# Value products as two 64-column halves and output transposes as four 64x64 tiles, in a delta-rule plus mixture-attention kernel

## Chip, core and metric

The kernel runs on one core of one Trainium2 chip, as one launch. Times are device microseconds. The time before is the median of three runs.

## What is computed

Inputs q, k, v have shape (4 batches, 8 heads, 768 positions, 48), beta (4, 8, 768). The first stage is a recurrence per batch and head (k normalized, state 48x48), the second a mixture of four causal attentions whose weights come from a top-2 gate:

```python
for t in range(S):                       # delta rule, per batch and head
    y[t] = q[t] @ state
    state = state + beta[t] * outer(k_n[t], v[t] - k_n[t] @ state)
x = y with the heads side by side        # (4, 768, 384)
logits = x @ w_gate                      # (384, 4), the two largest chosen
for e in range(4):
    q, k, v = x @ wq[e], x @ wk[e], x @ wv[e]      # 64 wide
    a = exp(causal(q @ k.T / 8) - rowmax); a /= a.sum() + 1e-9
    out += gate[e] * (a @ v @ wo[e])     # gate 0 where e was not chosen
```

## The kernel before

The work is cut into six units (n = 0 to 5): two batches at a time, three stretches of 256 positions each. s = n % 3 is the place of the stretch in the sequence, so attention in a unit covers s + 1 stretches of keys and the units grow: 0, 1, 2, then again 3, 4, 5 for the other two batches.

A unit goes through these stages. The recurrence is done in chunks of 64 positions: Gram products of keys (`gk`, `gq`), a triangular solve done step by step on VectorE and GpSimd (`pre`, `sv`, lines 420 and 422), then per chunk `ks`, `ex`, `uu`, `eu`, `yu`, `yq`, `st`, `es`. Those small products use the TensorE array as four 64x64 tiles in turn, in the order of rows and columns (0,0), (1,1), (0,1), (1,0). The outcome x is kept transposed in `xh`. The projections `pj` and `pv` are 128x128 products. The attention of a unit is, per batch b, pair of experts y and key stretch kp:

- `mx`, `em`: scores with queries as rows, for the row maxima; `mp`, `mr`, `er` turn the maxima over.
- `sc`: scores with keys as rows and queries as columns, in PSUM; the two experts of a pair are the two row halves of the array (64x128 tiles).
- `xp`: the exponential on ScalarE (line 743) into one of three tiles `at` (128 keys x 2 experts x up to 512 columns of queries).
- `av`: the product by values. The stationary operand is a 128x128 block of `at` (keys x queries), the moving one the 128x65 block of values `vs` (64 columns and a column of ones, which gives the row sum). The result, 128 queries x 65, is accumulated over key blocks in one PSUM bank, for two experts x and two query halves i side by side.
- `oa` copies the sums out to `os`, `nm` (line 760 on) turns row sums and gates into factors, `on` (line 765) multiplies.
- `ft`: transposes of `on` by a product with an identity, so that queries lie in columns; row half r of the queries goes to PSUM bank r. `fh`, `fl` split the result into a rounded part and a rest, `fo` applies wo in three 128x128 products, `eo` and `do` send it out.

Both `at`, `vs` and `on` are plain float32 tiles. A float32 product shows in the profile as two matmuls and two weight loads, so the 336 products of `av` are 672 and the 96 of `ft` are 192. The products that read float32r tiles (`pj`, `pv`, `sc`, `mx`, `fo`) show once.

The order of all steps on every engine is written out by hand in one long list of words, `ORDER`; each word calls one function with its arguments, the last digit after the colon being the PSUM buffer (four buffers of two banks). TensorE, VectorE, ScalarE and GpSimd each take their instructions in that order. All products go through one helper, `mm` (line 182), so that in the profile they are told apart by their tiles: `ps<-vs,at` is `av`, `ps<-cst,on` is `ft`, `ps<-kq` is `gk` and `gq`, `ps<-on,os` is a step of the first unit's solve that uses two 64x64 tiles in turn, rows 0-63 with columns 0-63 and rows 64-127 with columns 64-127.

In the order, the steps `av` form 27 groups on TensorE. Six of them follow, and seven precede, a step of full 128x128 products (`pj`, `pv`, `fo`, `fill`); the other neighbours use half tiles.

Of the kernel before, what the change touches and what calls it, by code (L numbers as in the profile page):

```python
# [23 lines left out]
SIDES = (slice(0, 64), slice(64, 128))  # L24
# [148 lines left out]
def tile_kernel(ctx, tc, kq, kv, beta, wqk, wvg, wo, consts, out):  # L173
# [7 lines left out]
    def mm(o, a, b, start, stop=True):  # L181
        T.matmul(o, lhsT=a, rhs=b, start=start, stop=stop, skip_group_check=True)  # L182
# [14 lines left out]
    def two(k):  # L197
        return PP[int(k)]
# [15 lines left out]
    id64 = cst[:, 0:64]  # L214
# [19 lines left out]
    VS = cp.tile([128, 2, 6, NE, EH + 1], F32, name="vs")  # L234
# [12 lines left out]
    ON = cp.tile([128, 2, NE, EH], F32, name="on")  # L247
# [415 lines left out]
    FOUR = ((0, 0), (1, 1), (0, 1), (1, 0))  # L663
# [81 lines left out]
    def av(n, b, y, kp, k):  # L745
        s = n % 3
        A = at_of(n, b, y, kp)
        O = two(k)[:, 0, 0:260].rearrange("p (x i d) -> p x i d", x=2, i=2)
        for j in range(2):
            for x in range(2):  # L750
                for i in range(j if kp == s else 0, 2):
                    o = 256 * j + 128 * i - (128 if kp == s and j else 0)
                    mm(O[:, x, i], A[:, x, o:o + 128], VS[:, b, 2 * kp + j, 2 * y + x], kp == j == x == i == 0)

    def oa(n, b, y, e, k):
        cpy(e, OS[b][:, 2 * y:2 * y + 2].rearrange("p x i d -> p (x i d)"), two(k)[:, 0, 0:260])
# [11 lines left out]
    def ft(n, b, k):  # L768
        for i in range(2):
            for x in range(2):  # L770
                for r in range(2):
                    w = 128 * i + 64 * x
                    mm(two(k)[:, r, w:w + 64], ON[SIDES[r], i, 2 * x:2 * x + 2].rearrange("p e d -> p (e d)"), id64[SIDES[r]], True)

    fv = lambda k: two(k)[:, :, 0:256].rearrange("p r (q t) -> p q r t", q=4)
    ov = lambda x: x.rearrange("p i x (r t) -> p (i x) r t", r=2)
# [103 lines left out]
```

## Time and profile before

| | |
|---|---|
| median of 3 runs | 488.77 us (484.72 to 489.02) |
| the profiled execution's own time | 488.29 us |
| its span, first to last instruction | 486.4 us |
| TensorE matmuls, busy | 433.9 us, 9543 instructions |
| VectorE, ScalarE, GpSimd busy | 313.6, 182.3, 170.8 us |
| mean granted TensorE clock | 0.959 |

"PE" is TensorE's matmul stream and "PEld" its weight loads; the two overlap. A group's busy time is the union of its instructions, while the length of one matmul is mostly latency, since matmuls are pipelined: the pace of a stream is read from the starts. The timeline view merges neighbouring instructions of one kind: "start, length, engine, line, operation, tiles, shape, count", and "128*128" ahead of a shape is the part of the array in rows * columns.

### The profile page before, as it was taken

Reading aid. Unit: us, or ns where it says so; the run is one execution under the profiler, and the core shown is the slowest. Engines: PE = TensorE matmul, PEld = TensorE weight load, DVE = VectorE, ACT = ScalarE, POOL = GpSimd, SP = SyncE. Lnnn points to the kernel's source line nnn. Section 1 sums busy time; section 2 is a strip of 40 time slices with the busy share of each in tenths; the row PEclk is TensorE's granted clock in tenths of the full one; section 3 lists DMA queues with packets and bytes.
Section 4 is the critical chain, followed back from the end, with each engine's and each line's share of the span. In section 5 each row is a group of like instructions: output and inputs, shape, how many; then the busy total and the mean of one; then the engine's idle time right before and its main releaser. Section 6 shows DMA issues by size and latency. Waiting matters only on the chain.

```text
span 486.4 us, 21099 instructions
## 1 busy us (share of the span) xinstructions
PE 433.9 (89%) x9543; PEld 396.1 (81%) x9543; DVE 313.6 (64%) x655; ACT 182.3 (37%) x349; POOL 170.8 (35%) x314
## 2 busy tenths in 40 slices
PE   5529888878999889998999999999999989999995
PEld 4529777867888769897888989999887879999994
DVE  3996769766679894776667485775677764642011
ACT  2516233532325542364352354173531122323331
POOL 1505744544474462404146342744601000011000
PEclk9999999868999996998699999999999989999999
DMA  8920343211303151120035120011403000000001
GB/s 187 236 71 13 91 119 102 49 36 47 105 11 107 34 167 52 52 67 1 3 100 150 35 53 1 1 36 37 144 16 110 19 3 18 2 34 15 20 1 66
DMA packets 15435, 29.33 MB, mean 60 GB/s; under 512 B 2801, under 2 KB 8945, under 8 KB 15345
## 3 DMA queue, kind: packets, MB, share of 16 engines
q1 hardware_dynamic: 15088, 27.59, 20.7%
q8 instruction: 75, 1.23, 1.1%
q10 hardware_dynamic: 256, 0.39, 0.3%
q14 instruction: 16, 0.12, 0.1%
HBM read 20.89 MB, written 4.72 MB: 53 GB/s over the span
## 4 chain that ended last, share of the span: by engine, by line
PE 71%; DVE 15%; DMA 4%; ACT 4%; issue 3%; SPq 1%; POOL 1%; DVEq 0%; ACTq 0%; POOLq 0%
PE ps L182 71%; DMA at<-in_wvg_dram 2%; ACT tt L186 1%; DVE bl L420 1%; DVE mx L684 1%; DVE tp L422 1%; DMA kq<-in_kq_dram 1%; DMA kv<-in_kv_dram 1%; DVE tn L452 1%; DVE ql L619 1%; SPq L596 1%; DMA xh<-xh 1%; DVE tt L190 1%; DVE xb L538 1%; DVE xh L590 1%
## 5 line engine op out<-in xcount | busy, mean ns | idle before, releaser
L182 PE MATMUL ps<-vs,at 128*128 128x65 f32 x672 | 80.1, 276 | 0.1
L182 PEld LDWEIGHTS ps<-vs,at 128*128 128x128 f32 x672 | 77.3, 192 | 1.8 <-ACT at L743 0.4
L422 POOL TENSOR_TENSOR tp<-bl 128x238 f32<-128x238 f32 (+13 forms) x90 | 44.0, 489 | 89.3 <-DVE bl L420 80.6
L743 ACT ACTIVATE at<-ps 128x768 f32<-128x768 f32 (+1 forms) x48 | 43.8, 919 | 50.0 <-PE ps L182 49.8
L684 DVE TENSOR_REDUCE mx<-ps 128x2 f32<-128x1024 f32 (+3 forms) x48 | 44.8, 952 | 13.9 <-PE ps L182 13.6
L420 POOL TENSOR_TENSOR bl<-bl,tp 128x238 f32<-128x238 f32 (+13 forms) x90 | 47.1, 523 | 7.1
L182 PE MATMUL ps<-kq 48*64 48x64 f32 x1536 | 38.2, 243 | 12.0 <-DVE tt L348 4.8
L182 PE MATMUL ps<-xh,wqkh 128*128 128x256 f32 x288 | 45.5, 294 | 2.9 <-DMA xh<-xh 1.8
L182 PEld LDWEIGHTS ps<-kq 48*64 48x64 f32 x1536 | 32.4, 154 | 16.0 <-issue 6.6
L182 PEld LDWEIGHTS ps<-xh,wqkh 128*128 128x128 f32 x288 | 38.6, 194 | 4.9 <-issue 2.0
L186 ACT ACTIVATE tt<-ps 32x256 f32<-32x256 f32 (+2 forms) x87 | 33.4, 384 | 17.1 <-PE ps L182 10.7
L182 PE MATMUL ps<-qh,kh 64*128 64x256 f32 x192 | 35.1, 357 | 1.1 <-DVE sb L562 1.1
L182 PE MATMUL ps<-kh,qh 64*128 64x512 f32 (+3 forms) x128 | 26.8, 439 | 3.5 <-DVE kl L619 2.1
L182 PE MATMUL ps<-ql,kh 64*128 64x256 f32 x192 | 28.2, 285 | 0.0
L182 PEld LDWEIGHTS <-ide 64*128 64x128 bf16 (+1 forms) x479 | 23.3, 103 | 5.9 <-issue 1.2
L182 PE MATMUL ps<-qh,kl 64*128 64x256 f32 x192 | 28.0, 283 | 0.0
L182 PE MATMUL ps<-mr,sel 64*128 64x256 bf16 x192 | 27.3, 276 | 0.0
L182 PE MATMUL ps<-wvgh,xh 128*128 128x260 f32 x144 | 25.4, 303 | 1.4 <-DVE pm L356 1.4
L182 PE MATMUL ps<-mask,ide 64*128 64x128 bf16 (+1 forms) x384 | 26.4, 217 | 0.0
L765 POOL TENSOR_TENSOR on<-os,rsm 128x512 f32<-128x512 f32 x9 | 9.4, 1048 | 46.1 <-DVE rsm L762 46.1
L182 PE MATMUL ps<-xh,wqkl 128*128 128x256 f32 x144 | 25.4, 286 | 0.0
L182 PEld LDWEIGHTS ps<-wvgh,xh 128*128 128x128 f32 x144 | 21.2, 204 | 2.0 <-DVE pm L356 1.6
(197 smaller groups left out, 915.9 us busy)
## 6 DMA issues: line engine op xcount, KB each, us to landing
kv<-in_kv_dram SPq DMA_DIRECT2D x24, 384.0 KB, 3.7
kq<-in_kq_dram SPq DMA_DIRECT2D x40, 192.0 KB, 3.6
out_dram<-ot SPq DMA_DIRECT2D x12, 384.0 KB, 2.9
xh<-xh SPq DMA_DIRECT2D x72, 32.0 KB, 2.5
kq<-in_kq_dram SPq DMA_DIRECT2D x12, 96.0 KB, 3.9
at<-in_wqk_dram SPq DMA_DIRECT2D x3, 256.0 KB, 3.8
kq<-in_kq_dram ACTq DMA_DIRECT2D x4, 96.0 KB, 4.0
at<-in_wvg_dram SPq DMA_DIRECT2D x1, 256.0 KB, 7.6
```

Of the source, the lines that this page charges most:

```text
L182: T.matmul(o, lhsT=a, rhs=b, start=start, stop=stop, skip_group_check=True)
L186: S.activation(o, x, AF.Copy, **({} if scale is None else {"scale": scale}))
L190: V.tensor_scalar(o, x, scale, None, op0=OP.mult)
L420: e.tensor_tensor(X[:, a:b, i + 1:], X[:, a:b, i + 1:], tv, op=OP.subtract)
L422: e.tensor_tensor(tv, R[:, :, i + 1:].to_broadcast([128, w, m]), X[:, a:b, i:i + 1].to_broadcast([128, w, m]), op=OP.mult)
L452: V.transpose(TN[n % 2].rearrange("p t l -> p l t"), BB[n % 2])
L538: V.tensor_tensor(XB.rearrange("p (a b) d -> p a (b d)", a=2), kv_of(n, c)[:, 1].rearrange("p (a b) d -> p a (b d)", a=2), ax(k), op=OP.su ...
L590: V.tensor_tensor(x, y, yv(n, c, k, 0)[0], op=OP.subtract)
L596: nc.sync.dma_start(x[r + HD:r + 64, :, i].bitcast(F32), x[r + 16 * i:r + 16 * i + 16, :, 3].bitcast(F32))
L684: V.tensor_reduce(d, two(k)[:, :, a:a + 128 * (k1 - k0)], axis=AX.X, op=OP.max)
L743: S.activation(at_of(n, b, y, kp)[:, :, 0:w], two(k)[:, :, 0:w], AF.Exp, scale=0.125)
L765: (V, G)[e - 1].tensor_tensor(ON, OS[b][:, :, :, 0:EH].rearrange("p e i d -> p i e d"), rsm[:, b, :, :, None].to_broadcast([128, 2, NE, EH ...
```

## The change

`av` loads 64 columns of `at` at a time instead of 128: each former product becomes two, of which one writes partitions 0-63 and the other partitions 64-127 of the same PSUM columns. Both use all 128 rows and the same moving block of values. `ft` transposes one expert's 64 columns at a time instead of two experts' 128, in the order of tiles `FOUR` = (0,0), (1,1), (0,1), (1,0) that the small products use already. `SIDES` are the slices 0:64 and 64:128. Results, their places, the other steps and `ORDER` stay.

```diff
@@ def av(n, b, y, kp, k)
-                    o = 256 * j + 128 * i - (128 if kp == s and j else 0)
-                    mm(O[:, x, i], A[:, x, o:o + 128], VS[:, b, 2 * kp + j, 2 * y + x], kp == j == x == i == 0)
+                    for c in range(2):
+                        o = 256 * j + 128 * i + 64 * c - (128 if kp == s and j else 0)
+                        mm(O[SIDES[c], x, i], A[:, x, o:o + 64], VS[:, b, 2 * kp + j, 2 * y + x], kp == j == x == i == 0)
@@ def ft(n, b, k)
-                for r in range(2):
+                for r, c in FOUR:
                     w = 128 * i + 64 * x
-                    mm(two(k)[:, r, w:w + 64], ON[SIDES[r], i, 2 * x:2 * x + 2].rearrange("p e d -> p (e d)"), id64[SIDES[r]], True)
+                    mm(two(k)[SIDES[c], r, w:w + 64], ON[SIDES[r], i, 2 * x + c], id64[SIDES[r]], True)
```

## The prediction

> **What bounds the kernel now.** I read the page first: the span, the engines, the clock, the chain that ended last, and the groups of the value product.
>
> ```profile
> span 486.4 us, 21099 instructions
> PE 433.9 (89%) x9543; PEld 396.1 (81%) x9543; DVE 313.6 (64%) x655; ACT 182.3 (37%) x349; POOL 170.8 (35%) x314
> PEclk9999999868999996998699999999999989999999
> PE 71%; DVE 15%; DMA 4%; ACT 4%; issue 3%; SPq 1%; POOL 1%; DVEq 0%; ACTq 0%; POOLq 0%
> L182 PE MATMUL ps<-vs,at 128*128 128x65 f32 x672 | 80.1, 276 | 0.1
> L182 PEld LDWEIGHTS ps<-vs,at 128*128 128x128 f32 x672 | 77.3, 192 | 1.8 <-ACT at L743 0.4
> ```
>
> TensorE is busy 89% of the span and carries 71% of the chain, and the value product alone holds 80 us of it, nearly without idle time ahead of it. A mean says nothing of where, so the next view is the busy time by stage. The columns are length, then busy time and count of PE, PEld, DVE, ACT and POOL, then clock and DMA; the last row is the end of the chain's view in order of time.
>
> ```profile
> 115.00:200.00 85.00, 77.28 (x1875) 69.14 (x1876) 65.63 (x138) 35.59 (x76) 45.62 (x82) 0.94 0.25 70
> 200.00:350.00 150.00, 146.18 (x3111) 134.59 (x3110) 102.21 (x223) 64.86 (x119) 65.04 (x117) 0.97 0.18 50
> 350.00:394.00 44.00, 39.34 (x1062) 35.15 (x1060) 30.28 (x61) 12.27 (x24) 4.35 (x4) 1.00 0.21 57
> 394.00:476.00 82.00, 82.00 (x1018) 76.88 (x1019) 30.24 (x59) 25.23 (x34) 6.55 (x18) 0.98 0.06 18
> ...
> 393.94 82.09 PE ps L182 x1014
> ```
>
> From 394 to 476 us TensorE is never idle, the chain is one unbroken piece on it, and VectorE and ScalarE are busy only 30 and 25 of 82 us. Time taken from TensorE there should reach the end. From 200 to 350 TensorE has 3.8 us of idle time, but VectorE is busy 68%. From 115 to 200 VectorE has 77%.
>
> The same stages, for the matmuls of the value product (three rows, `vs`) and of the output transposes (four rows, `on` with its identity in `cst`):
>
> ```profile
> 115.00:200.00 85.00, 6.95 (x59) 0.94 0.25 70
> 200.00:350.00 150.00, 39.23 (x327) 0.97 0.18 50
> 394.00:476.00 82.00, 33.95 (x288) 0.98 0.06 18
> ...
> 115.00:200.00 85.00, 2.22 (x32) 0.94 0.25 70
> 200.00:350.00 150.00, 6.53 (x96) 0.97 0.18 50
> 394.00:476.00 82.00, 3.17 (x48) 0.98 0.06 18
> 476.00:486.40 10.40, 1.11 (x16) 0.90 0.11 39
> ```
>
> Half of the value product lies in the middle, two fifths in the unbroken stretch, none from 350 to 394.
>
> **What one product costs, and what half of one will.** Pace is (length of a merged row minus the length of one matmul) over (count minus one). The timeline gives the rows, the views by tile the lengths (min/median/max):
>
> ```profile
> 427.88 4.68 PE L182 MATMUL ps<-vs,at 128*128 128x65 f32 x40
> 310.75 1.11 PE L182 MATMUL ps<-cst,on 64*128 64x64 f32 x16
> 41.89 1.10 PE L182 MATMUL ps<-on,os 64*64 64x64 f32 x32
> 340.71 0.66 PE L182 MATMUL ps<-kq 48*64 48x64 f32 x32
> ...
> L182 PE MATMUL ps<-vs,at x672: 218/275/324, 122.6 to 475.7; 128*128 128x65 f32 x168
> L182 PE MATMUL ps<-cst,on x192: 218/272/320, 145.3 to 478.8; 64*128 64x64 f32 x192
> L182 PE MATMUL ps<-on,os x64: 218/218/267, 41.9 to 62.2; 64*64 64x64 f32 x64
> L182 PE MATMUL ps<-kq x1536: 213/218/367, 3.7 to 371.0; 48*64 48x64 f32 x192
> ```
>
> - Value product, 128 columns loaded: (4.68 - 0.275) / 39 = 113 ns.
> - Transposes, 64x128 in two row halves: (1.11 - 0.272) / 15 = 55.9 ns, so 112 ns per row half, and both halves run at once.
> - Two 64x64 tiles in turn, (0,0) and (1,1): (1.10 - 0.218) / 31 = 28.5 ns, so 57 ns per tile.
> - Four 64x64 tiles in turn: (0.66 - 0.218) / 31 = 14.3 ns, so again 57 ns per tile.
>
> Two things follow. At the same 64 or 65 moving columns, a pass takes 112 ns with 128 stationary columns and 57 with 64, whatever the rows: the weight load sets the pace and hides the product. And four tiles keep 57 ns each, although (0,0) and (0,1) share their rows: two column halves do load and multiply at once. If the tiles of one row half took turns, four could not beat 28.5 ns.
>
> **The change part by part.** *Value product.* 672 matmuls of 113 ns, 75.9 us, become 1344. The trace has no 128-row tile of 64 columns. Nearest row: two tiles in turn, 28.5 ns. I take 29 ns for 65 columns in place of 64: 39.0 us, 37 us less, or 55 ns per old matmul. Bounds: 14.3 ns (19 us in all) if a tile of 128 rows ran as the four do, which I exclude since only two tiles are open; above, 57 ns if the column halves take turns (76.6 us, no gain) and 114 if a load also stops the other half's product. By stage: 59, 327 and 288 matmuls give 3.2, 18.0 and 15.8 us.
>
> *Transposes.* 192 matmuls of 55.9 ns become 384 of 14.3, a row of the trace itself: 27.3 ns per old one, 5.2 us; by stage 0.9, 2.6, 1.3 and 0.4.
>
> *Number of instructions.* The four-tile row issues a load and a matmul each 14.3 ns, so 29 ns is no issue limit. Both halves write the same PSUM bank at other partitions, as the four tiles of `gk` do. The copies that follow wait for the last half, as before. No wait, DMA or tile is added.
>
> *Switches of the array's tiling.* Today `av` sits in the same tiling as `fo`, `pj`, `pv`. What a switch costs stands in these pairs, `av` to `fo` and `av` to a 64x128 product:
>
> ```profile
> 440.38 2.00 PE L182 MATMUL ps<-vs,at 128*128 128x65 f32 x16
> 442.19 0.60 PE L182 MATMUL ps<-woh,oh 128*128 128x384 f32 x2
> ...
> 316.26 1.89 PE L182 MATMUL ps<-vs,at 128*128 128x65 f32 x16
> 318.09 0.23 PE L182 MATMUL ps<-ide,mp 64*128 64x64 bf16 x4
> ```
>
> The last `av` matmul starts one length (0.275) before its row ends: 442.105 and 317.875. The next starts 0.085 and 0.215 us later, so a switch costs 0.13. By the order, 6 groups of `av` follow full products and 7 precede them: 13 new switches, 1.7 us, of which about 1.0 from 394 on. Around the transposes eight switches go and seven come: nothing. If no drain shows, 1.7 us more are gained.
>
> *What passes through.* After 394: 15.8 + 1.3 - 1.0 = 16.1 us; I take 15, as VectorE and ScalarE would be busy 30 and 25 of some 66 us. I followed the dense stretch from 450 on in the timeline; its tightest place is `ft` behind GpSimd's `on`:
>
> ```profile
> 458.69 1.04 POOL L765 TENSOR_TENSOR on<-os,rsm 128x512 f32<-128x512 f32 x1 [14.64 <-DVE rsm L762]
> 461.30 1.00 PE L182 MATMUL ps<-cst,on 64*128 64x64 f32 x16
> ```
>
> It ends at 459.73, 1.57 us ahead of its reader. Between the `av` that `on` waits for and `ft` lies one group of 16 value products, which gives up 16 x 55 ns = 0.9 us: the wait stays covered. The tail gives its 0.4. From 200 to 350: 18.0 + 2.6 - 0.7 = 19.9 us; the 102 us of VectorE would then fill 79% of 130, and in a fixed order some short product waits for a VectorE step that was hidden: I take two thirds, 13. From 115 to 200: 4.1 us, but VectorE is busy 65.6 of 85 there: 1.6. From 350 to 394: nothing. Sum 30.0. The profiled execution took 488.29, close to the median of 488.77, so 488.3 - 30 = 458.3.
>
> **A rule against it.** The pace above has loads of one column half under products of the other. The Trainium skill, "TensorE: Matmul & The Clock Gate", Part 3, "The mechanism", says that weight loads overlap with products in flight only where the row groups differ; the two halves of `av` share theirs. Taken so, the change would be the last rival below. The trace speaks against it: `av` today, all in one row group, has 113 ns for a load and a product together, while its 64-column cousins need 57.
>
> **The clock.** TensorE runs at half speed after it has been idle. Two idle stretches and what followed (clock is the third column from the end):
>
> ```profile
> 226.00:228.00 2.00, 0.82 (x5) 0.30 (x4) 1.28 (x2) 1.85 (x5) 2.00 (x1) 1.00 0.00 0
> 228.20:238.40 10.20, 9.94 (x155) 8.73 (x156) 6.65 (x13) 4.13 (x11) 4.40 (x12) 0.51 0.01 2
> ...
> 392.00:394.00 2.00, 0.19 (x6) 0.06 (x4) 1.58 (x5) 0.60 (x1) 0.00 (x0) 1.00 0.01 4
> 395.50:398.90 3.40, 3.40 (x56) 2.64 (x52) 2.40 (x3) 1.02 (x1) 0.00 (x0) 0.52 0.00 0
> ```
>
> A long episode costs half of 10.2 us, 5 us. A faster TensorE idles more, so one more may come, or one may fall elsewhere: plus or minus 5 us, put into the range.
>
> **The rivals.** *Other engines take over.* VectorE's 68 to 77% before 350 is a mean over stretches that are full; the middle keeps a quarter (5 us), the end 12, the start nothing: 17.4 us with the tail, 471 (466 to 476). For it: the order was laid out for the old lengths. Against it: TensorE is busy 97% in the middle. *All of it passes:* 4.1 + 19.9 + 16.1 + 0.4 = 40.5, 448, and 443 with one slow-clock episode less. For it: the unbroken piece. *The halves take turns*, so the change doesn't do what it says: `av` 0.7 us longer, 1.7 for switches, about 4 of 5.2 gained on the transposes: 487. Only the four-tile row speaks against it, and its tiles have 64 rows. *Slower:* at 128 rows a load of one half stops the product of the other, at each of the 1344 passes: 57 + 57 = 114 ns, 153 us in place of 76, and with TensorE the bound nearly all shows: 488.3 + 77 + 1.7 - 4 = 563. It decides from about 58 ns per matmul: (75.9 + 4 - 1.7) / 1344.
>
> **How the numbers follow.** Forecast 458 (own range 450 to 466): 0.57. Other engines, 471: 0.20. All passes, 448 or less: 0.13. Turns, 487: 0.05. Stops, 563: 0.03; the rest, 0.02, is slower clock that eats the gain. The range 446 to 474 holds the forecast, most of the second and half of the third. A change within 1% is about what a measurement of this kernel can't tell from none. Faster: 0.57 + 0.20 + 0.13 = 0.90; same 0.06; slower 0.04.
>
> **What would show it.** `ps<-vs,at` 128*64 x1344 at about 29 ns from start to start, some 45 us busy; `ps<-cst,on` 64*64 x384 at 14 to 15; a gap near 0.2 us between `av` and `fo`; the last stretch, from its first unbroken piece to the last `av`, some 67 us; more TensorE waits on VectorE before 350. The prediction falls if the pace is near 57 ns or above, if TensorE's idle time grows by more than 15 us, or if half-clock episodes add up to twice their share.

## Result and profile after

The changed kernel took 451.58 us (median of 4 runs, 450.39 to 456.18); the kernel before, beside it, 487.78 (4 runs, 484.72 to 489.02). The ratio is 0.928 with a 95% interval of 0.920 to 0.937, so 36 us were gained, where 30 were forecast. Some runs of one kernel come out 1.5% or more above its fastest one; the ratios in this document leave these out, the medians don't. The profiled execution took 452.6 us itself, 35.7 less than the one of before.

From the page of the changed kernel, the lines that answer to the first five shown of before, and the group of the value product:

```profile
span 450.9 us, 22827 instructions
PE 392.5 (87%) x10407; PEld 352.6 (78%) x10407; DVE 313.7 (70%) x655; ACT 182.0 (40%) x349; POOL 171.3 (38%) x314
PEclk9999999988899998899799999999999898999999
PE 67%; DVE 16%; DMA 6%; ACT 5%; issue 4%; POOL 1%; SPq 0%; DVEq 0%; ACTq 0%
L182 PE MATMUL ps<-vs,at 128*64 128x65 f32 x1344 | 45.2, 224 | 0.0
L182 PEld LDWEIGHTS ps<-vs,at 128*64 128x64 f32 x1344 | 41.4, 138 | 2.9 <-issue 0.8
```

The work of the other engines is unchanged to within 1 us. TensorE lost 41.4 us of busy time, 34.9 of them in the value product (80.1 to 45.2) although it has twice the instructions. "issue", time in which an engine waited for nothing that the profile shows, went from 3% to 4% of the chain; more on that below.

The pace, as before from the timeline and from the lengths in the views by tile:

```profile
424.96 2.79 PE L182 MATMUL ps<-vs,at 128*64 128x65 f32 x88
402.98 0.69 PE L182 MATMUL ps<-cst,on 64*64 64x64 f32 x32
403.60 2.55 PE L182 MATMUL ps<-vs,at 128*64 128x65 f32 x80
406.08 0.61 PE L182 MATMUL ps<-woh,oh 128*128 128x384 f32 x2
427.68 0.39 PE L182 MATMUL ps<-qh,kh 64*128 64x256 f32 x2
...
L182 PE MATMUL ps<-vs,at x1344: 219/222/272, 118.9 to 440.6; 128*64 128x65 f32 x192
L182 PE MATMUL ps<-cst,on x384: 217/218/267, 139.5 to 443.3; 64*64 64x64 f32 x192
```

Value product: (2.79 - 0.222) / 87 = 29.5 ns, where 113 stood. Transposes: (0.69 - 0.218) / 31 = 15.2 ns, where 55.9 stood.

Where the time went, by the chain in order of time; the first piece is the unbroken stretch that was 82.09 us long, the rest is the tail:

```profile
373.38 67.50 PE ps L182 x1344
440.90 0.44 DVE os L188
442.08 0.70 DVE on L766
442.82 1.46 PE ps L182 x40
444.29 2.40 PE ps L182 x12
```

From that and the rows of before (first value product at 122.6 and now 118.9, start of the stretch at 393.94 and now 373.38, its end at 476.06 and now 440.90), the 35.5 us of span divide so:

| stretch | before | after | difference | forecast |
|---|---|---|---|---|
| start to first value product | 122.6 | 118.9 | -3.7 | 0 |
| from there to the unbroken stretch | 271.3 | 254.5 | -16.9 | -14.6 |
| unbroken stretch | 82.1 | 67.5 | -14.6 | -15 |
| tail | 10.3 | 10.0 | -0.3 | -0.4 |

The first row can't come of the change: no changed instruction runs there. In the twelve profiled runs of this study the first value product starts between 117.1 and 127.2 us: before 120 us in the four whose clock was at half speed for 10 us ahead of it, later in the eight where it was for 14 to 23 us. So this row is chance.

The middle could have given 24 us of TensorE time (19.9 and 4.1 in the forecast's sums) and gave 16.9. TensorE's busy time there did fall by 24.0 us, from 256.8 to 232.8, but its idle time grew by 7.1, from 14.6 to 21.7. What TensorE's matmuls waited for in that part, before (122 to 394 us) and after (119 to 380 us), "us in total, times, longest":

```profile
PE ps L182 <- DVE mp L702: 1.8, 1, 1.8
PE ps L182 <- DVE pm L356: 1.4, 1, 1.4
PE ps L182 <- DVE sb L562: 1.4, 2, 1.1
PE ps L182 <- issue: 1.3, 3, 0.7
...
PE ps L182 <- issue: 7.7, 7, 1.7
PE ps L182 <- DVE mp L702: 1.8, 1, 1.8
PE ps L182 <- DVE pm L356: 1.4, 1, 1.4
PE ps L182 <- DVE xh L590: 1.3, 2, 0.8
```

The first four lines are of before, the others of after, each time with the longest waits on VectorE: those hardly changed (9.7 us before and 9.8 after, over all waits on VectorE). What grew, by 6.4 of the 7.1 us, is waiting with no releaser.

**The theory after the result.** Loads set the pace, the two column halves load and multiply at once, and the gain passes. The middle's shortfall is a shortage of instructions: TensorE now takes them in faster than they are brought. The page counts them as a DMA queue of their own, 75 packets before and 81 after, 16 KB each. After the change 20814 loads and matmuls go with 81 packets, 257 to a packet; the text reckons with 256, that is 128 pairs of load and matmul:

```profile
q8 instruction: 75, 1.23, 1.1%
...
q8 instruction: 81, 1.33, 1.2%
```

In the single records of this queue (the trace's start and end of every packet) successive packets land 3.3 to 4 us apart when TensorE is starved, 26 to 31 ns for a pair. Steps in four tiles use up a pair each 14 to 15 ns. Until the change the value product, at 113 ns a pair, let the supply catch up; at 29.5 ns, about the pace of the supply itself, it doesn't. The rivals: that the halves need not alternate, the smaller load being all; that VectorE and the solve bound the middle; and that the waits without a releaser belong to certain steps.

### The profile page after: what moved, and what is told of

It reads as the page before. It is cut to its first block, busy times and chain, and to the rows that moved or that the text cites. A ratio compares the mean times of both kernels' runs of the same rounds, so it can differ in the third digit from the quotient of the medians.

```text
span 450.9 us, 22827 instructions
## 1 busy us (share of the span) xinstructions
PE 392.5 (87%) x10407; PEld 352.6 (78%) x10407; DVE 313.7 (70%) x655; ACT 182.0 (40%) x349; POOL 171.3 (38%) x314
## 4 chain that ended last, share of the span: by engine, by line
PE 67%; DVE 16%; DMA 6%; ACT 5%; issue 4%; POOL 1%; SPq 0%; DVEq 0%; ACTq 0%
PE ps L182 67%; DMA kq<-in_kq_dram 6%; DVE tn L452 2%; ACT tt L186 1%; ACT bl L186 1%; DVE ql L619 1%; DVE xh L590 1%; DVE mx L684 1%; DVE bl L360 1%; DVE tt L190 1%; DVE pm L356 1%; ACT qh L186 1%; DVE tn L436 1%; DVE sb L562 1%; DVE gc L653 1%
## 5 line engine op out<-in xcount | busy, mean ns | idle before, releaser
L182 PE MATMUL ps<-vs,at 128*64 128x65 f32 x1344 | 45.2, 224 | 0.0
L182 PEld LDWEIGHTS ps<-vs,at 128*64 128x64 f32 x1344 | 41.4, 138 | 2.9 <-issue 0.8
L422 DVE TENSOR_TENSOR tp<-bl 128x210 f32<-128x210 f32 (+14 forms) x60 | 21.4, 357 | 3.0 <-POOL bl L420 2.1
L420 DVE TENSOR_TENSOR bl<-bl,tp 128x210 f32<-128x210 f32 (+14 forms) x60 | 21.6, 360 | 2.1
```

The costliest lines, as they stand in the source:

```text
L420: e.tensor_tensor(X[:, a:b, i + 1:], X[:, a:b, i + 1:], tv, op=OP.subtract)
L422: e.tensor_tensor(tv, R[:, :, i + 1:].to_broadcast([128, w, m]), X[:, a:b, i:i + 1].to_broadcast([128, w, m]), op=OP.mult)
```

## Experiments

**Each part alone.** The diff of the change, split in two: `av` alone, then `ft` alone.

> Only the value product is cut into column halves; the transposes stay as before. Theory (the weight load sets the pace, both halves at once, most of it passes through): pace of the value product 29 to 30 ns, PE busy near 396 us, time 455 to 458, that is 4 us above the full change, as the transposes' 5.2 us of TensorE time are the only difference. Rival (the transposes' 192 more matmul-and-load pairs cost in instruction supply what they save on the array): the same as the full change or below it, 449 to 452.

> Only the transposes go to 64x64 tiles; the value product stays at 128 columns. Theory: 384 matmuls at 14 to 15 ns, 5.2 us less TensorE time, of which 3 to 4 pass: 484 to 485. Rival (shorter transposes only wait for what follows): 487 to 489, no difference.

Value product alone: 453.77 us (4 runs, 450.41 to 456.37) against 487.55 (13 runs of before), ratio 0.937 (0.927 to 0.947), a gain of 26 to 36 us. Transposes alone: 482.18 (10 runs), ratio 0.994 (0.988 to 1.000), between nothing and 6 us; their busy time fell from 13.1 to 8.2. The value product's time lies between what theory (455 to 458) and rival (449 to 452) gave, and that of the transposes below both ranges, which were reckoned from a time before of 488.8. The value product is nearly all of the change. Beside it the transposes bring 1 to 2 us (the full change took 451.58 and, below, 453.03), less than these runs can tell.

**The order of the halves.** All products of one half ahead of those of the other, within each step:

```diff
-        for j in range(2):
-            for x in range(2):
-                for i in range(j if kp == s else 0, 2):
-                    for c in range(2):
+        for c in range(2):
+            for j in range(2):
+                for x in range(2):
+                    for i in range(j if kp == s else 0, 2):
```

> The full change, but within a step all products of the first column half come ahead of all those of the second, so that neighbours share their half of the array; the count of instructions and their work are those of the full change. Theory (the gain is that two halves load at once): 57 ns from start to start, 76 us for the value product, and nearly the old time, 484 to 489. Rival (the gain is the smaller load alone, or loads are taken ahead far enough that the order does not matter): 29 to 30 ns, 450 to 455.

476.47 us (474.19 to 481.32), ratio 0.983 (0.969 to 0.996): 23 to 25 us slower than the full change with the same instructions. From its page and timeline:

```profile
L182 PE MATMUL ps<-vs,at 128*64 128x65 f32 x1344 | 73.0, 227 | 0.1
443.88 4.46 PE L182 MATMUL ps<-vs,at 128*64 128x65 f32 x88
```

(4.46 - 0.222) / 87 = 48.7 ns instead of 29.5. In the single records the starts lie mostly 58 to 59 ns apart inside a half; where the halves change, some three passes of either run side by side, which brings the mean below 57 and fits a time 8 us under the expected range. So the gain is not the smaller load as such: alternating neighbours run at once. In the full change two halves start 6 to 8 ns apart, and the next two some 52 ns later.

**Four tiles, twice the instructions.** The same work with rows halved too, the second row half into the second PSUM bank, which this kernel leaves out of the sums that follow:

```diff
-        O = two(k)[:, 0, 0:260].rearrange("p (x i d) -> p x i d", x=2, i=2)
+        O = two(k)[:, :, 0:260].rearrange("p r (x i d) -> p r x i d", x=2, i=2)
...
-                    for c in range(2):
+                    for r, c in FOUR:
                         o = 256 * j + 128 * i + 64 * c - (128 if kp == s and j else 0)
-                        mm(O[SIDES[c], x, i], A[:, x, o:o + 64], VS[:, b, 2 * kp + j, 2 * y + x], kp == j == x == i == 0)
+                        mm(O[SIDES[c], r, x, i], A[SIDES[r], x, o:o + 64], VS[SIDES[r], b, 2 * kp + j, 2 * y + x], kp == j == x == i == 0)
```

> The value product in four 64x64 tiles, the two row halves into two PSUM banks; the second bank's share is left out of the sums that follow. 2688 matmuls with as many loads in place of 1344. If the array alone counts, they run at 14.3 to 15 ns, 38 to 40 us in all, and the time is that of the full change within 2 us. If the supply of instructions counts (in the changed kernel's trace a 16 KB packet of 256 TensorE instructions lands each 3.3 to 4 us at best, 128 matmul-and-load pairs, 26 to 31 ns for one pair), these steps fall to about 29 ns a pair when the supply is used up, waits of TensorE with no releaser grow from 12 to over 20 us, and the time is 5 to 15 us above the full change: 457 to 467.

470.35 us (465.35 to 472.61), 17 to 19 us above the full change and 3 above the range given. Group of the value product, one of its runs broken in two, and the waits from 119 to 390 us:

```profile
L182 PE MATMUL ps<-vs,at 64*64 64x65 f32 x2688 | 47.3, 220 | 4.9 <-issue 4.7
255.93 1.63 PE L182 MATMUL ps<-vs,at 64*64 64x65 f32 x96
259.16 1.34 PE L182 MATMUL ps<-vs,at 64*64 64x65 f32 x77 [1.60 <-issue]
...
PE ps L182 <- issue: 20.1, 20, 1.7
```

(1.63 - 0.218) / 95 = 14.9 ns while instructions last: the array needs no more time than with two halves (2688 x 14.9 = 40 us). The waits without a releaser in the middle go from 7.7 us in 7 to 20.1 in 20, some of them inside a step, where no semaphore is waited for. Twice the instructions for the same work on the array cost 17 to 19 us by the medians. Of the two profiled executions this one took 465.35 us, 12.8 more than the 452.6 of the full change, and these waits account for 12.4; why the medians lie further apart no run here shows.

**The supply by itself.** 32 more Gram steps behind the last step:

```diff
         fns[f](*args, *rest)
+
+    for z in range(32):
+        gq(5, 3, 1)
```

> The full change with 32 more Gram steps of one chunk (four 64x64 tiles in turn, no engine reads them) behind the last step of TensorE: 1024 pairs of a load and a matmul in one run without waits. If the array alone counts, each pair takes 14.3 to 15.4 ns throughout, 15 us in all. If the supply of instructions counts, the first 150 to 300 pairs do so and the rest run at 26 to 31 ns on the mean, in bursts with gaps that have no releaser: 22 to 30 us in all.

471.48 us. The run of 1024 pairs in the timeline; in brackets the idle time ahead and what ended it:

```profile
442.93 4.19 PE L182 MATMUL ps<-kq 48*64 48x64 f32 x271
448.54 2.09 PE L182 MATMUL ps<-kq 48*64 48x64 f32 x128 [1.42 <-issue]
452.29 3.29 PE L182 MATMUL ps<-kq 48*64 48x64 f32 x128 [1.65 <-issue]
455.76 5.73 PE L182 MATMUL ps<-kq 48*64 48x64 f32 x256 [0.18 <-issue]
462.97 2.09 PE L182 MATMUL ps<-kq 48*64 48x64 f32 x128 [1.48 <-issue]
466.99 1.86 PE L182 MATMUL ps<-kq 48*64 48x64 f32 x113 [1.93 <-issue]
...
452.80:459.60 6.80, 6.62 (x250) 6.44 (x244) 0.00 (x0) 0.00 (x0) 0.00 (x0) 0.50 0.02 5
```

The first 271 pairs take (4.19 - 0.218) / 270 = 14.7 ns each. From then on the pieces have 128 or 256 pairs, that is 16 or 32 KB of instructions, with idle time between. All 1024 take 25.9 us, 25 ns a pair. Not all of that is supply: after the first two waits the clock was at half speed for 6.8 us (last row, columns as in the prediction's tables), the pairs there start 26.7 ns apart, as slowly as they are brought, and the wait ahead of the piece of 256 is only 0.18 us. At full speed the array would have needed 3.4 us less there; the waits are 6.7 us in all. The pace of the supply is read from wait to wait: from 448.54 to 466.99 us 640 pairs run, 28.8 ns each. In the records, the seven packets that land meanwhile come 3.3 to 4.0 us after one another, 26 to 31 ns a pair. The expectation held, with no wait of the program in sight.

**The stages apart.** The value product in halves in the last two units (`n >= 4`), then in the first four (`n < 4`), transposes as before:

```diff
-                    o = 256 * j + 128 * i - (128 if kp == s and j else 0)
-                    mm(O[:, x, i], A[:, x, o:o + 128], ...)
+                    for c in range(2 if n >= 4 else 1):
+                        o = 256 * j + 128 * i + 64 * c - (128 if kp == s and j else 0)
+                        P, w = (O[SIDES[c], x, i], 64) if n >= 4 else (O[:, x, i], 128)
+                        mm(P, A[:, x, o:o + w], ...)
```

> The value product is cut into halves in the last two units alone (288 of the 672 old matmuls, those from 394 us on in the trace before); transposes and the other units as before. Theory (there TensorE is the only bound, all of it passes): 15 us less than before, 471 to 474, and one unbroken piece of TensorE to the last value product that is 14 to 16 us shorter than the 82.1 us of before. Rival (VectorE's maxima or ScalarE's exponentials take over): 8 us or less, 479 or above.

> The value product is cut into halves in the first four units alone (384 old matmuls, 21 us of TensorE time); transposes and the last two units as before. Theory (two thirds to four fifths pass, as TensorE is the bound between the waits of the solve): 14 to 18 us less than before, 470 to 474. Rival (VectorE and the solve set the pace before 394 us): 5 us or less, 482 or above. With the run on the last two units it should add up to what the value product gave alone, 34 us, within 4.

Last two units: 472.96 us (468.01 to 474.62) against 489.30, ratio 0.968 (0.955 to 0.981). Its unbroken stretch:

```profile
392.56 68.06 PE ps L182 x1303
```

14.0 us shorter than 82.09, as expected. First four units: 465.34 (464.60 to 476.57), ratio 0.955 (0.945 to 0.964), a gain of 17 to 27 us where 14 to 18 were expected. The rival, VectorE and the solve as the bound, said 5 or less and is out. The two gains, 16 and 22 us, sum to 38, the value product alone gave 31 by its ratio (34 by medians): not within the 4 us asked for in the ratios, but inside what their intervals allow.

**Moving the packets' edges.** 64 more filling products where TensorE waits for the first solve:

```diff
-zx.0.0.0 fill.8:1 zp.1.0:1
+zx.0.0.0 fill.72:1 zp.1.0:1
```

and beside it the full change once more, and the full change with the old transposes in the first four units:

```diff
-                for r, c in FOUR:
+                for r, c in FOUR if n >= 4 else ((0, 0), (1, 0)):
                     w = 128 * i + 64 * x
-                    mm(two(k)[SIDES[c], r, w:w + 64], ON[SIDES[r], i, 2 * x + c], id64[SIDES[r]], True)
+                    if n >= 4:
+                        mm(two(k)[SIDES[c], r, w:w + 64], ON[SIDES[r], i, 2 * x + c], id64[SIDES[r]], True)
+                    else:
+                        mm(two(k)[:, r, w:w + 64], ON[SIDES[r], i, 2 * x:2 * x + 2].rearrange("p e d -> p (e d)"), id64[SIDES[r]], True)
```

> The full change once more, for its spread: 450 to 456. Theory of the instruction supply: TensorE's waits without a releaser in the middle fall on the same steps as before (near the counts of pairs k + 0.5 packets of 128), in any run.

> The full change with 64 more filling products while TensorE waits for the first unit's solve (they fit into 8.4 us of idle time), which moves every later step by half a packet of 128 pairs. Supply theory: the waits without a releaser leave their steps and lie again at k + 0.5 packets of the new count, that is on steps 64 pairs earlier in the program; their sum and the time may go up or down by up to 5 us, 447 to 457. Rival (these waits belong to the steps, a wait that the profile does not show): they stay on the same steps, and the time is that of the full change less 1 us for a warm clock at the first solve products.

> The full change, but the transposes of the first four units stay at 64x128 (128 pairs of instructions fewer, 3.5 us more of TensorE time where the supply is short), those of the last two units go to 64x64. Supply theory: the waits without a releaser fall by 2 to 6 us, which pays for the 3.5 us: 449 to 453, no worse than the full change. Rival (the array's time alone counts): 3 us above the full change, 454 to 456.

| kernel | median us (lowest to highest) | ratio to before, 485.24 |
|---|---|---|
| full change again | 453.03 (450.70 to 459.56) | 0.935 (0.930 to 0.939) |
| 64 fillers more | 450.76 (448.16 to 456.94) | 0.930 (0.925 to 0.935) |
| old transposes in four units | 454.94 (452.16 to 463.77) | 0.938 (0.932 to 0.945) |

The waits without a releaser of 0.4 us and more behind the first value product, counted in the records as pairs since the start over 128 (the one in brackets, 0.76 us long, is put down to VectorE's `xh` in the view):

```
full change, first run    25.62  31.59 (44.54) 47.54  58.52  60.51  67.46
full change, second run   25.62  31.59  44.54  47.54  58.52  60.51  67.46
64 fillers more           31.59  32.59  37.57  44.54  45.54  59.52  61.51
```

All lie near half a packet, in each kernel, and the same kernel has them at the same places in both runs. Without the fillers one is within a step `gq` or `gk` (first row); with them this step runs through, and the wait lies half a packet further on in the program (further back was expected), between two matmuls of one `fo` product (second row):

```profile
313.19 0.63 PE L182 MATMUL ps<-kq 48*64 48x64 f32 x28 [1.29 <-issue]
...
316.04 0.44 PE L182 MATMUL ps<-woh,oh 128*128 128x384 f32 x1 [1.12 <-issue]
```

So they belong to the packets, not to the steps. The landings say the same. In the twelve profiled runs there are 79 such waits, and every one ends 1.2 to 1.7 us after a packet of TensorE's instructions has landed; the number of packets landed by then is each time the whole number in front of the half, 25 at 25.62 and 31 at 31.59. Of the 172 other waits of that length behind the first value product 16 end so. TensorE thus stands still until the next packet is there, and half a packet on this scale is the edge of one.

The version with fillers is the fastest run, but its interval overlaps that of the full change: no proof of a gain. With the old transposes in the middle the waits there fall from 7.7 to 4.0 us, as the supply theory has it; the time, 454.9, lies in the rival's range and above the supply theory's 449 to 453, but the intervals of 454.9 and 453.0 overlap. Whether the shorter waits paid back the 3.5 us of array time stays open.

## Why the prediction held, point by point

- **Pace.** 29 ns was taken from two tiles in turn, 29.5 measured; the transposes' 14.3 came out at 15.2. Both follow from reading that 112 ns per 128 columns and 57 per 64 mean a load that hides its product. At 64 columns the product is no longer the shorter part: see the last section.
- **Both halves at once.** This was inferred from four 64-row tiles and is now shown for 128 rows: 58 ns inside a half, 29.5 in alternation. The Trainium skill, "TensorE: Matmul & The Clock Gate", Part 3, "The mechanism", has loads overlap products in flight only where the row groups differ; that does not hold here, where both halves use all rows. The same section of the Trainium skill also lets a load go ahead into a background weight buffer, which no run here tells apart. The Trainium skill, "TensorEngine Tiling (Array Packing)", "Key Properties", has different tiles load and multiply in parallel, which agrees with the runs.
- **Switches of tiling, mis-sized.** The last value product before `fo` starts at 403.60 + 2.55 - 0.222 = 405.93, `fo` at 406.08: 0.15 us, where 0.085 stood and 0.215 was forecast. Leaving to a 64x128 tile, 427.68 after 424.96 + 2.79 - 0.222, also takes 0.15, where 0.215 stood. The forecast put the same price on the way in, but the single records have another: behind a full product the first value product started 0.12 us after the start of the last `pj` or `pv` and 0.17 after that of `fo`, now 0.21 and 0.27, so 0.09 more. Seven times 0.07 and six times 0.09 are 1.0 us in place of 1.7; and the 20 groups that leave to half tiles save 0.055 each (0.205 before, 0.15 now), 1.1 in all. The term of 1.7 us is about nothing.
- **The last stretch.** 15 us forecast, 14.6 in the full change, 14.0 for the value product alone there.
- **The middle.** 14.6 us forecast, 16.9 measured in the profiled pair, 17 to 27 in the run of the first four units. That not all of 24 us passes was right; the reason was wrong, so that the size came near is luck. VectorE's waits did not grow; waits for instructions did, by 6.4 us. The step that failed is "some short product waits for a VectorE step that was hidden", and with it the sentence that 29 ns is no issue limit: it looked at the shortest pace in a row of 32, not at what a long run can keep up.
- **The level.** 458 against 451.6: in the profiled pair 3.7 us of the 6 lie before the first value product, in the spread from run to run, and 2.3 in the middle. By the mean clocks, 0.959 of 486.4 us and 0.964 of 450.9, TensorE was at half speed for 40 us before and 32 after. Half of the difference, some 3.7 us, is an estimate of what the clock gave beside the change, so the better part of the excess over the forecast may be chance. The bound of 5 us for the clock was of the right size.
- **The rivals.** Turns (487) is what the order of the halves decides, 476 when they don't alternate; the last rival, loads that stop the other half, would have meant 114 ns and is excluded. That all passes (448) and that others take over (471) lie on either side of the 451.6 measured.

## What to carry to other kernels

Where a float32 product has few moving columns, compare rows with 128 and 64 stationary columns: if the pace halves, the load is the bound, and two column halves in alternation carry the same work in half the time. Put the alternation in the innermost loop. Then count instructions: a change that doubles them can move the bound to their supply, which shows as idle time with no releaser, in steps that have nothing to wait for.

## What the hardware showed beyond that

TensorE's instructions arrive in packets of 256, not closer than 3.3 to 4.0 us in the starved runs, 26 to 31 ns a pair of load and matmul, while four tiles can run a pair in 14.7. Stores ahead lasted for 271 pairs in the long run; then came waits of 1.4 to 1.9 us, and one of 0.2 where the clock was at half speed. All 79 waits without a releaser of 0.4 us and more, over twelve runs, end 1.2 to 1.7 us behind the landing of a packet; what takes that time, and why packets don't land closer, no run here shows. The Trainium skill, "Runtime: NRT & Kernel Launch", "Instruction fetch mechanics", has the refill in 16 KB blocks, which agrees, and calls its cost mostly hidden, which the long run contradicts.

At 64 stationary and 64 moving columns the load and the product of a plain float32 tile take equally long. In the single records of the kernel before, four tiles in turn start 14.2 ns apart with 48 stationary and 64 moving columns (`ps<-pm,ub`), 14.5 with 64 and 48 (`ps<-sb,kq`), and 11.6 with 48 and 48 (`ps<-ub,kv`): the larger of the two counts sets the pace. So blocks of 32 stationary columns would, by these rows, leave a tile's pace as it is; no run here tried them.
